# Two levels of 7-product multiplication for half of the gates in the last two groups, with the weight sums streamed from memory and the second sums of x made by GpSimd

## The chip, the core and the metric

The kernel runs on one core of a Trainium2 chip. A core has five engines that run side by side and wait for each other through semaphores: TensorE (PE in the profile, PEld for its weight loads), VectorE (DVE), ScalarE (ACT), GpSimd (POOL) and SyncE (SP, which here only issues transfers). The metric is the device time of one execution, in microseconds (us). Before the change the median of 3 executions was 768.82 us (767.99 to 770.23).

## The reference

```python
kv = einsum('bhsd,bhse->bhde', k, v)  # per batch and head: k^T v      (8 batches, 8 heads, 576 rows, 64 wide)
o  = q @ kv
x  = o / sqrt(mean(o*o) + 1e-6) * g  # then reshaped to 4608 rows x 512
a  = x @ w1                          # 512 -> 1024
b  = x @ w2                          # 512 -> 1024
h  = (a * b) @ w3                    # 1024 -> 1024
out = h @ w_out                      # 1024 -> 512
```

All values are float32. The two products `x @ w1` and `x @ w2` with the multiplication after them are called the gates here, and what follows them the projection; the kernel folds `w3 @ w_out` into one 1024 x 512 matrix at its start, so the projection is one product.

## The kernel before

**Groups.** The 4608 rows are worked on in nine groups of 512. Groups `T` = 0 to 7 hold 512 rows of batch `T`; group 8 holds the 64 rows left over of each batch. The order is 0, 1, ..., 6, 8, 7 (line 1100). For each group the gates are made in four blocks `p` = 0 to 3 (`gates`, line 742; each block is 128 features of the lower and 128 of the upper half, for w1 and w2), and then the projection (`project_twice`, line 859; group 0 uses `project`). Beside the gates of group `T` the attention of batch `T+1` is worked off in pieces (`steps`, called through `between`, line 1104), so the last two groups, 8 and 7, have no attention beside them.

**One level of 7 products.** A product of two matrices cut into 2 x 2 blocks can be made from 7 block products instead of 8, at the price of sums of blocks before and after. `winograd` (line 610) does so: the sums of weights s1 to s4 (`sums`), the sums of x t1 to t4 (`combine`) and the 7 products in the order (a11,b11), (s1,t1), (s2,t2), (s4,b22), (s3,t3), (a12,b21), (a22,t4). A block product of the gates is 4 matmuls of 128 x 128 weights by 256 rows (w1 and w2, two chunks of the contraction each), so a block `p` is 28 matmuls. The profile counts each float32 matmul as two instructions. `keep` (line 628) is ScalarE's copy of a product from PSUM to SBUF; `multiply` (line 747) adds two results on VectorE (line 756) and multiplies the two gates (line 757); the last result goes through a ScalarE copy and line 753. After each block, `sum_ab` (line 729) makes four sums of the finished gates, `ab`, for the projection (lines 670 and 671).

**Two levels in the projection.** `project_twice` cuts each of the 7 products again into 7: `sum_inner(n)` (line 844, lines 852 to 856) makes four sums of a left-hand block, `products(n)` (line 872) issues 7 x 2 matmuls of 128 x 128 by 128, and the results are kept (lines 905, 906), added (lines 933, 934, and 987) and finished on VectorE (`finish`, lines 915 to 918: one instruction of 128 elements a partition, three of 256). The second-level sums of the right-hand matrix were written to memory once by `prepare_b`, during group 1; `load_b` brings the 7 parts (896 KB each) of every group into three buffers in turn (`streams`), each as soon as the part three before it was used.

**Order.** TensorE, GpSimd and SyncE issue in the order of the program's text. VectorE does so from the last block of the gates to the end of the projection (`in_order`, line 1123); elsewhere the framework's scheduler orders VectorE and ScalarE. Each engine works strictly in its order, so an instruction that waits holds up all behind it. The chain that opens the projection is `following` (line 1114): after the result "c11" of block 3, VectorE makes the sums `sum_inner(0)`, which `products(0)` needs.

**Single buffers.** The tiles "p1", "p5", "u" (u2, u3 and u4 share it), "c" and "c21" of `late_pool` exist once each: a new `keep` into "u" waits until VectorE has read what is there. PSUM has five banks for "mm" and three for "at".

Of the kernel before, what the change touches and what calls it, by code (L numbers as in the profile page):

```python
# [2 lines left out]

# [8 lines left out]
FP32 = mybir.dt.float32  # L12
# [9 lines left out]
def kernel(  # L22
# [32 lines left out]
    nc = tc.nc  # L55
    PSUM = bass.MemoryType.PSUM
    P = 128

    B, H, S, D = q.shape
    DM = H * D  # L60
    DF = w1.shape[1]
    NP = H // 2
    KF = DF // P
    NH = KF // 2
    J = 4
    G = J * P
    N = G // 2
# [4 lines left out]
    const = ctx.enter_context(tc.tile_pool(name="const", bufs=1))  # L72
    inp = ctx.enter_context(tc.tile_pool(name="inp", bufs=2))
    work = ctx.enter_context(tc.tile_pool(name="work", bufs=2))
    ps_mm = ctx.enter_context(tc.tile_pool(name="ps_mm", bufs=5, space=PSUM))
    ps_at = ctx.enter_context(tc.tile_pool(name="ps_at", bufs=3, space=PSUM))
# [5 lines left out]
    def bank(pool, tag):  # L82
        return pool.tile([P, 512], FP32, name=tag, tag=tag)
# [31 lines left out]
    NF = KF // 2  # L115
# [141 lines left out]
    eps_col = const.tile([P, 1], FP32, name="eps_col")  # L257
    nc.vector.memset(eps_col, 1e-6)

    kv_sb = [const.tile([P, 2, NP, D], FP32, name=f"kv_sb{i}") for i in range(2)]  # L260
    g_col = const.tile([P, 1], FP32, name="g_col")


# [340 lines left out]
    late = {}  # L604
    tick = const.tile([P, 1], FP32, name="tick")

    def late_tile(name):
        return late_pool.tile([P, 7, P], FP32, name=name[0] if name[0] == "u" else name)
# [65 lines left out]
    def run(*step_lists):  # L674

        for steps in zip(*step_lists):
            for step in steps:
                step()
# [5 lines left out]
    PART = 7 * 2 * P  # L684
# [32 lines left out]
    def combine_x(T):  # L717
        xb[T] = {f"b{i + 1}{j + 1}": xT[T][:, i, j] for i in range(2) for j in range(2)}
        return combine(xb[T], parts(xc))
# [9 lines left out]
    def sum_ab(p):  # L729
        aa[p] = {f"a{i + 1}{j + 1}": ab[j][:, p, i, :] for i in range(2) for j in range(2)}  # L730
        return sums(aa[p], free["ab", p])
# [10 lines left out]
    def gates(T, p, between, ready=lambda name: None):  # L742
        def done(name, one, two):
            multiply(name, one, two)
            ready(name)

        def multiply(name, one, two):

            dst = ab[int(name[1]) - 1][:, p, int(name[2]) - 1, :]
            if two is None:  # L750
                c = late_pool.tile([P, N], FP32, name="c21")
                nc.scalar.copy(c, one[:, 0, :])
                nc.vector.tensor_mul(dst, c, one[:, 1, :])
                return
            c = late_pool.tile([P, 2, N], FP32, name="c")
            nc.vector.tensor_add(c, one, two)  # L756
            nc.vector.tensor_mul(dst, c[:, 0, :], c[:, 1, :])  # L757

        winograd(
            lambda name, w, c: wa[p][name][:, w, c, :],  # L760
            lambda name, c: xb[T][name][:, c, :],
            NP // 2, done, between,
        )


    def project(T, between):
        def done(name, one, two):
            half, j = int(name[1]) - 1, int(name[2]) - 1
            dst = o_sbs[half][:, :, j * N:(j + 1) * N]
            if two is None:  # L770
                nc.scalar.copy(dst, one)
            else:
                nc.vector.tensor_add(dst, one, two)
            if name in ("c11", "c21"):
                rows = out[T * S:T * S + G, :].rearrange("(p j) f -> p j f", j=J)
                nc.sync.dma_start(out=rows[:, 2 * half:2 * half + 2, :], in_=o_sbs[half])

        winograd(
            lambda name, m, p: aa[p][name][:, m * P:(m + 1) * P],
            lambda name, p: ob[p][name],  # L780
            NF, done, between,
        )
# [12 lines left out]
    def prepare_b():  # L795

        nc.sync.dma_start(
            out=w3o_l2[7, :, 0:1024].rearrange("p (f n) -> p f n", n=N), in_=b_blocks()[5]
        )
        for n, y in enumerate(b_blocks()):  # L800
            b11, b12, b21, b22 = (
                y[:, 2 * i:2 * i + 2, j * P:(j + 1) * P] for i in range(2) for j in range(2)
            )


            stage = w3o_sums[0].rearrange("p f n -> p (f n)") if n == 4 else (
                o_sbs[(n - n // 5) % 2].rearrange("p m n -> p (m n)")
            )
            stage = stage[:, 0:6 * P]
            t1, t2, t4 = (t.rearrange("p (c n) -> p c n", n=P) for t in (  # L810
                stage[:, i * 2 * P:(i + 1) * 2 * P] for i in range(3)
            ))
            nc.vector.tensor_sub(t1, b12, b11)
            nc.vector.tensor_sub(t2, b22, t1)
            nc.vector.tensor_sub(b12, b22, b12)
            nc.vector.tensor_sub(t4, b21, t2)
            nc.sync.dma_start(
                out=w3o_l2[n, :, 0:1024].rearrange("p (f n) -> p f n", n=N), in_=y
            )
            nc.sync.dma_start(out=w3o_l2[n, :, 1024:PART], in_=stage)  # L820
            yield
# [4 lines left out]
    def load_b():  # L826
        n = len(loaded_b)
        if n == ALL_B:
            return
        t = streams[n % len(streams)]  # L830

        part = {ALL_B - 2: 6, ALL_B - 1: 7}.get(n, n % 7)

        queue = nc.scalar if n % 7 in (3, 5) else nc.sync
        if n + 1 < ALL_B:
            queue.dma_start(out=t, in_=w3o_l2[part])
        else:
            t = t[:, 0:1024]
            queue.dma_start(out=t, in_=w3o_l2[part, :, 0:1024])
        loaded_b.append(t)  # L840
# [15 lines left out]
        nc.vector.tensor_sub(a21, a11, a21)  # L856
        inner[n] = [a11, a12, a22, s1, s2, s4, a21]

    def project_twice(T, last, ahead):
        def store(half):  # L860
            if T < B:
                rows = out[T * S:T * S + G, :].rearrange("(p j) f -> p j f", j=J)
# [118 lines left out]

            add(p5, r1)
        z = keep("u3", r1)
        load_b()
        if not last:
            sum_inner(6)
            nc.vector.tensor_add(p5, p5, z)
        finish(p5, 1, 1)
        products(6 if last else 5, r2)
        load_b()  # L990
        if last:
            add(z, r2)
            finish(z, 1, 0)
            last_block()
        else:
            add(p1, r2)
            finish(p1, 0, 0)
            products(6, r1)
            load_b()
            finish(keep("u4", r1), 1, 0)  # L1000

    done = {}
    dram = ctx.enter_context(tc.tile_pool(name="dram", bufs=1, space=bass.MemoryType.DRAM))
    w3o_l2 = dram.tile([8, P, PART], FP32, name="w3o_l2")


    ctx.enter_context(tc.manual_schedule(
# [93 lines left out]
    for n, T in enumerate(groups):  # L1101
        pieces = steps(T + 1) if n + 2 < NG else iter([])

        def between():
            next(pieces, lambda: None)()
            if T == 1:
                for _ in range(2):
                    if next(preparing, 0) == 0 and len(loaded_b) < 3:
                        load_b()

        for p in range(NF):
            if T and p + 1 == NF:
                sum_1, sum_2, sum_4, sum_3 = sum_ab(p)
                following = {
                    "c12": [], "c22": [sum_1],
                    "c11": [
                        lambda: sum_inner(0, lambda: all_of(f() for f in (sum_2, sum_3))),
                        lambda: sum_inner(1),
                    ],
                    "c21": [sum_4],  # L1120
                }

                in_order = tc.manual_schedule(engines={mybir.EngineType.DVE})
                in_order.__enter__()
                gates(T, p, between, lambda name: all_of(f() for f in following[name]))
                continue
            gates(T, p, between if T or p else lambda: None)
            if T == 0:
                if p + 1 < NF:
                    run(sum_w(p + 1))  # L1130
                for n in range(2):
                    if len(converted) < len(todo):
                        ahead = [copies["xT"] if p == 0 else copies["u3"][0], copies["u2"][p]][n]
                        with tc.issue_after(ahead.ins):
                            begin_next()
                        end_next()
                if p + 1 == NF:
                    allocate_projection()
                    run(*(f(i) for i in range(NF) for f in (sum_ab, combine_w3o)))
            else:  # L1140
                run(sum_ab(p))
        last = n + 1 == NG
        if T:
            project_twice(T, last, [] if last else combine_x(groups[n + 1]))
            in_order.__exit__(None, None, None)
            continue
        project(T, between)
        run(combine_x(1))
        preparing = prepare_b()
        third = late_pool.tile([P, 3, 2, P], FP32, name="inner_sums")  # L1150
        inner_sums.append([third[:, i] for i in range(3)])

# [29 lines left out]
```

## Time and profile before

| | |
|---|---|
| median of 3 executions | 768.82 us (767.99 to 770.23) |
| the profiled execution | 767.41 us |
| its span, first to last instruction | 765.4 us |
| TensorE busy | 758.5 us (99%), granted clock 0.999 |
| VectorE busy | 543.9 us (71%) |
| ScalarE busy | 253.3 us (33%) |
| GpSimd busy | 136.6 us (18%), none of it in the last two groups |
| gates of one block in the last two groups | 12.09 us |
| projection of one group (98 matmuls) | 21.89 us |

The page of a profile gives busy time by engine, the span in slices, the chain of work that ended last, and the costliest groups of instructions by source line. The timeline lists instructions in order of time: start, duration, engine, line, output and inputs, and in brackets the idle time of the engine before it with what ended it. A table of windows gives the busy time of each engine in stretches of the span. A matmul's shown duration is longer than the distance to the next one, since matmuls are pipelined; costs of TensorE are taken from the distance. On VectorE too the next instruction may start a little before the one ahead has ended, when it doesn't need its result.

### The profile page before, as it was taken

The page shows a single profiled execution, that of the slowest core. Times are in us where ns is not written, and L with a number is a line of the kernel's source. Part 1 is how long each engine was busy: PE and PEld are TensorE (multiplying, and loading weights), DVE is VectorE, ACT ScalarE, POOL GpSimd, SP SyncE. Part 2 cuts the span into 40 slices and gives each one's busy share as a digit, 9 for nine tenths or more (in the row PEclk, how much of TensorE's full clock was granted, in tenths as well). Part 3 has the DMA queues.
Part 4 walks back from the last instruction along what each step waited for, and adds up shares of the span by engine and source line. Part 5 has one row for each costly group of instructions (what it writes and reads, how often), then busy time and mean ns, then how long its engine had stood idle before and what let it go on. Part 6 is the DMA issues. An engine that isn't in the chain of part 4 may idle for free.

```text
span 765.4 us, 14413 instructions
## 1 busy us (share of the span) xinstructions
PE 758.5 (99%) x5775; PEld 660.1 (86%) x5775; DVE 543.9 (71%) x1083; ACT 253.3 (33%) x479; POOL 136.6 (18%) x132
## 2 busy tenths in 40 slices
PE   8999999999999999999999999999999999999998
PEld 6455788888899889988998899889988998898897
DVE  7978999548878578756775787667765864495467
ACT  6677763213222332223222321232133222222221
POOL 0000000222610351043113511331144000000000
PEclk9999999999999999999999999999999999999999
DMA  9996641339997844873487448844852470065015
GB/s 320 337 340 196 195 141 40 84 91 261 332 292 253 227 115 119 273 214 97 128 272 200 117 137 267 190 111 128 284 101 47 134 258 1 1 234 158 1 35 193
DMA packets 133159, 132.55 MB, mean 173 GB/s; under 512 B 76644, under 2 KB 121188, under 8 KB 133092
## 3 DMA queue, kind: packets, MB, share of 16 engines
q1 hardware_dynamic: 130640, 116.81, 52.5%
q10 hardware_dynamic: 2452, 14.81, 5.7%
q8 instruction: 46, 0.75, 0.4%
q14 instruction: 21, 0.17, 0.1%
HBM read 100.27 MB, written 16.38 MB: 152 GB/s over the span
## 4 chain that ended last, share of the span: by engine, by line
PE 97%; DMA 1%; ACT 0%; issue 0%; SPq 0%; DVE 0%; ACTq 0%
PE mm L617 60%; PE mm L894 23%; PE mm L596 7%; PE at L332 3%; PE at L415 2%; DMA raw<-in_moe_w_out_dram 1%; PE at L583 1%; PE at L351 1%; PE at L945 0%; DMA raw<-in_moe_w_dram 0%; PE at L449 0%; PE at L434 0%; ACT ab L157 0%; ACT chunks L158 0%; ACT kv_sb L343 0%; PE mm L434 0%
## 5 line engine op out<-in xcount | busy, mean ns | idle before, releaser
L617 PE MATMUL mm<-xT,w_sb 128*128 128x256 f32 x768 | 176.2, 379 | 0.0
L617 PEld LDWEIGHTS mm<-xT,w_sb 128*128 128x128 f32 x768 | 145.5, 190 | 20.0 <-issue 0.5
L617 PE MATMUL mm<-xc,ws 128*128 128x256 f32 x576 | 130.2, 379 | 0.0
L617 PEld LDWEIGHTS mm<-xc,ws 128*128 128x128 f32 x576 | 109.3, 190 | 15.0
L756 DVE TENSOR_TENSOR c<-mm,u 128x512 f32<-128x512 f32 x36 | 24.8, 689 | 103.3 <-PE mm L617 103.3
L630 ACT COPY u<-mm 128x512 f32<-128x512 f32 x74 | 43.4, 587 | 137.8 <-PE mm L617 129.2
L630 ACT COPY p<-mm 128x512 f32<-128x512 f32 x74 | 43.4, 586 | 88.0 <-PE mm L617 86.0
L617 PE MATMUL mm<-xc,w_sb 128*128 128x256 f32 x288 | 69.0, 382 | 0.0
L290 POOL COPY xT<-xn 128x1024 uint16<-128x1024 uint16 x26 | 31.7, 1249 | 173.0 <-DVE xn L393 173.0
L894 PE MATMUL mm<-w3o_sb,raw 128*128 128x128 f32 x500 | 62.4, 276 | 0.0
L596 PE MATMUL mm<-chunks,ab 128*128 128x512 f32 x128 | 60.3, 603 | 1.3 <-ACT ab L588 0.7
L757 DVE TENSOR_TENSOR ab<-c 128x256 f32<-128x256 f32 x108 | 59.1, 547 | 3.0
L617 PE MATMUL mm<-xT,ws 128*128 128x256 f32 x256 | 61.1, 381 | 0.0
L617 PEld LDWEIGHTS mm<-xc,w_sb 128*128 128x128 f32 x288 | 53.9, 190 | 7.7 <-ACT u L630 0.3
L894 PEld LDWEIGHTS mm<-w3o_sb,raw 128*128 128x128 f32 x500 | 59.0, 192 | 0.4 <-DVE raw L852 0.2
L617 PEld LDWEIGHTS mm<-xT,ws 128*128 128x128 f32 x256 | 48.0, 190 | 6.6
L384 DVE TENSOR_REDUCE inv<-sq 128x8 f32<-128x512 f32 (+1 forms) x40 | 23.4, 627 | 37.7 <-ACT sq L383 37.7
L756 DVE TENSOR_TENSOR c<-p,u 128x512 f32<-128x512 f32 x36 | 26.5, 736 | 27.5 <-ACT u L630 27.4
L894 PE MATMUL mm<-w3o_sb,ab 128*128 128x128 f32 x336 | 43.7, 275 | 0.0
L596 PEld LDWEIGHTS mm<-chunks,ab 128*128 128x128 f32 x128 | 21.8, 190 | 23.8 <-issue 15.8
L905 ACT COPY u<-mm 128x512 f32<-128x512 f32 x23 | 13.5, 587 | 85.7 <-DVE raw L918 63.2
L894 PEld LDWEIGHTS mm<-w3o_sb,ab 128*128 128x128 f32 x336 | 41.0, 192 | 0.3
(162 smaller groups left out, 1149.1 us busy)
## 6 DMA issues: line engine op xcount, KB each, us to landing
w3o_sb<-w3o_l SPq DMA_DIRECT2D x26, 896.0 KB, 4.9
raw<-in_moe_w_dram SPq DMA_DIRECT2D x31, 512.0 KB, 7.5
raw<-w3o_l SPq DMA_DIRECT2D x13, 896.0 KB, 5.2
w3o_sb<-w3o_l ACTq DMA_DIRECT2D x11, 896.0 KB, 4.6
k_sb<-in_k_dram SPq DMA_DIRECT2D x32, 256.0 KB, 4.0
v_sb<-in_v_dram SPq DMA_DIRECT2D x32, 256.0 KB, 4.6
q_sb<-in_q_dram SPq DMA_DIRECT2D x32, 256.0 KB, 4.4
out_dram<-raw SPq DMA_DIRECT2D x14, 512.0 KB, 3.5
```

The source lines that it names most:

```text
L290: nc.gpsimd.tensor_copy(to, src.rearrange("p a n w -> p w a n"))
L332: nc.tensor.matmul(kv_ps[e * D:(e + 1) * D, r - rs[0], :], lhsT=k_sb[:, e, cols] if j < J else kl[:, 2 * r + e, :], rhs=v_sb[:, e, cols] i ...
L351: nc.tensor.transpose(qt_ps[:, e, i, :], q_sb[:, e, i * P:(i + 1) * P], ident)
L384: nc.vector.tensor_reduce(out=inv[:, i], in_=sq.rearrange("p (h d) -> p h d", d=D), axis=AX.X, op=ALU.add)
L415: nc.tensor.matmul(o_ps[l][tokens, n * D:(n + 1) * D], lhsT=qT[r][rows, e, i, tokens], rhs=kv_b[rows, e, r, :], start=True, stop=True,)
L596: nc.tensor.matmul(sums_ps[half][m], lhsT=w3T[half, c][:, m, :], rhs=chunks[:, c, 1, :], start=(c == 0), stop=(c == KF - 1),)
L617: nc.tensor.matmul(ps[:, u, :], lhsT=lhsT(a_name, u, c), rhs=rhs(b_name, c),  start=(u == 0 and c == 0 and to is None), stop=(c == chunks ...
L630: copies.setdefault(name, []).append(nc.scalar.copy(t, ps))
L756: nc.vector.tensor_add(c, one, two)
L757: nc.vector.tensor_mul(dst, c[:, 0, :], c[:, 1, :])
L894: nc.tensor.matmul(to[:, i, :], lhsT=x[:, c, :], rhs=y[:, c, :], start=new and place // 4 not in seen, stop=(c == 1), skip_group_check=True,)
L905: nc.scalar.copy(t[:, 0:4], ps[0])
```

## The change

In the last two groups (`TWICE` = 8 and 7), blocks 0 and 1 of the gates are made together by two levels of 7 products. The contraction, the features and the rows are cut a second time: `gates_of_two` issues, for w1 and then w2, 7 outer times 7 inner products of one matmul each (128 x 128 by 128): 98 matmuls in place of 56. Its results are kept, added and finished as in the projection; for w2 a product with w1's result is added to each `finish`. The order of the blocks in these groups becomes 2, (0 and 1), 3; `sum_ab(0)` and `sum_ab(1)` come after the pair, ahead of block 3, and VectorE keeps the text's order from the pair on.

The second-level sums are made as follows. Those of the weights, 3 for each of 7 products, are made once by VectorE in `prepare_w`, called from `between` in blocks 0 and 1 of groups 3 and 4, and written to memory by 21 transfers of 128 KB; the fourth overwrites a weight block in group 6 (`replace_a21`). `load_w` brings them back in three parts of 896 KB, in place of the last three `load_b` of groups 6 and 8; those three `load_b` move into `gates_of_two`. The second sums of x, 28 subtractions of 128 x 128 for each group, are made by GpSimd (`sum_x`) during block 2 of the group, into tiles that attention used before. Two attention tiles become one (`kv_two`), which serves as another "u".

In the order that the built program has, the sums of `prepare_w` for products 0 and 1 (in group 3) and for 4 and 5 (in group 4; two times 3 instructions) stand on VectorE between the `finish` instructions of the projection before; those for products 2 and 6 stand before the two reductions of the attention's norm, and those for product 3 after the first addition of block 1. The subtractions of `replace_a21` stand around the four results of block 1 of group 6.

```diff
-    kv_sb = [const.tile([P, 2, NP, D], FP32, name=f"kv_sb{i}") for i in range(2)]
+    kv_two = const.tile([P, 2, 2, NP, D], FP32, name="kv_two")
+    kv_sb = [kv_two[:, i] for i in range(2)]
...
+    def w_blocks(name):
+        return [wa[m][name][:, :, c, :] for m in range(2) for c in range(2)]
+
+    def prepare_w():
+
+        for n, (name, _) in enumerate(PRODUCTS):
+            a11, a12, a21, a22 = w_blocks(name)
+            s1, s2, s4 = inner_sums[2 * (n % 2)]
+            nc.vector.tensor_add(s1, a21, a22)
+            nc.vector.tensor_sub(s2, s1, a11)
+            nc.vector.tensor_sub(s4, a12, s2)
+            for i, s in enumerate((s1, s2, s4)):
+                at = (3 * n + i) * 2 * P
+                nc.sync.dma_start(
+                    out=w_l2[:, at:at + 2 * P].rearrange("p (w m) -> p w m", w=2), in_=s
+                )
+            yield
+
+    def replace_a21():
+        for name, _ in PRODUCTS:
+            a11, _, a21, _ = w_blocks(name)
+            nc.vector.tensor_sub(a21, a11, a21)
+
+    loaded_w = []
+
+    def load_w():
+        n = len(loaded_w)
+        t = streams[(len(loaded_b) + n) % len(streams)]
+        nc.sync.dma_start(out=t, in_=w_l2[:, n * PART:(n + 1) * PART])
+        loaded_w.append(t)
...
+    def sum_x(T):
...
+        nc.gpsimd.tensor_copy(tick, late["p1"][:, 0, 0:1])
+        for t, (_, name) in zip(x_sums, PRODUCTS):
+            b11, b12, b21, b22 = (
+                xb[T][name][:, c, i * P:(i + 1) * P] for c in range(2) for i in range(2)
+            )
+            t1, t2, t3, t4 = t
+            nc.gpsimd.tensor_sub(t1, b12, b11)
+            nc.gpsimd.tensor_sub(t2, b22, t1)
+            nc.gpsimd.tensor_sub(t3, b22, b12)
+            nc.gpsimd.tensor_sub(t4, b21, t2)
...
+    def gates_of_two(T):
...
+            for place, x, y in (
+                (0, a11, b11), (3, a12, b21), (1, a22, t4), (2, s1, t1), (6, s2, t2), (5, s4, b22),
+                (4, s3, t3),
+            ):
+                nc.tensor.matmul(
+                    ps[place // 4][:, place % 4, :], lhsT=x, rhs=y,
+                    start=new and place // 4 not in seen, stop=True, skip_group_check=True,
+                )
+                seen.add(place // 4)
+            if w == 1 and n in (2, 4, 6):
+                load_b()
+            return ps
...
+        def finish(z, w, i, j):
...
+            dst = ab[i][:, 0:2, j, :].rearrange("p m (n t) -> p m n t", t=P)
+            to = dst
+            if w:
+                to = late_pool.tile([P, 2, N], FP32, name="c").rearrange("p m (n t) -> p m n t", t=P)
+            nc.vector.tensor_add(z[:, 6], z[:, 6], z[:, 0])
+            nc.vector.tensor_add(z[:, 4:6], z[:, 4:6], wide(6))
+            nc.vector.tensor_add(to[:, 1], z[:, 1:3], wide(4))
+            nc.vector.tensor_add(to[:, 0], z[:, 3:6:2], z[:, 0:3:2])
+            if w:
+                nc.vector.tensor_mul(dst, dst, to)
+
+        for w in range(2):
+            one = places["p1"] if w else late_tile("p1")
+            r1 = products(0, w, banks(ps_mm, "mm"), True)
+            p1 = keep(one, r1)
+            r2 = products(1, w, banks(ps_mm, "mm"), True)
+            p5 = keep(late_tile("p5"), r2)
+            products(2, w, r1, False)
+            z = keep(late_tile("u2"), r1)
+            products(3, w, r2, False)
+            add(z, r2)
+            finish(z, w, 0, 1)
+            products(4, w, r1, False)
+            u3 = keep(places["u"], r1)
+            nc.vector.tensor_add(p5, p5, u3)
+            finish(p5, w, 1, 1)
+            r3 = products(5, w, banks(ps_at, "at"), True)
+            add(p1, r3)
+            finish(p1, w, 0, 0)
+            products(6, w, r1, False)
+            finish(keep(late_tile("u4"), r1), w, 1, 0)
+        loaded_w.clear()
...
-        load_b()
+        load_after()
...
+            if T in (3, 4) and p < 2:
+                next(preparing_w, 0)
+            if T == B - 2 and p == 2 and not replaced:
+                replaced.append(True)
+                replace_a21()
+
+        if T in TWICE:
+            once = iter([T])
+            gates(T, 2, lambda: [sum_x(t) for t in islice(once, 1)])
+            run(sum_ab(2))
+            in_order = tc.manual_schedule(engines={mybir.EngineType.DVE})
+            in_order.__enter__()
+            gates_of_two(T)
+            run(sum_ab(0), sum_ab(1))
         for p in range(NF):
+            if T in TWICE and p + 1 < NF:
+                continue
...
-            project_twice(T, last, [] if last else combine_x(groups[n + 1]))
+            project_twice(
+                T, last, [] if last else combine_x(groups[n + 1]),
+                load_w if not last and groups[n + 1] in TWICE else load_b,
+            )
```

## The prediction

> **What bounds the kernel now.** I read the page's busy times and chain first, then a table of windows of group 7, then the timelines of TensorE and VectorE there.
>
> ```profile
> span 765.4 us, 14413 instructions
> PE 758.5 (99%) x5775; PEld 660.1 (86%) x5775; DVE 543.9 (71%) x1083; ACT 253.3 (33%) x479; POOL 136.6 (18%) x132
> PE 97%; DMA 1%; ACT 0%; issue 0%; SPq 0%; DVE 0%; ACTq 0%
> ```
>
> TensorE is the bound: the chain is 97% TensorE, so a saved matmul is saved time as long as nothing makes TensorE wait. Who would, shows in the windows (columns: stretch, then busy time of PE, PEld, DVE, ACT, POOL); first group 8's projection, then group 7's blocks 0 to 2:
>
> ```profile
> 669.52:691.41 21.89, 21.89 (x198) 21.88 (x196) 20.82 (x51) 5.12 (x10) 0.00 (x0) 1.00 0.70 235
> 691.41:703.50 12.09, 12.09 (x59) 10.64 (x57) 6.39 (x15) 2.83 (x5) 0.00 (x0) 1.00 0.65 196
> 703.50:715.60 12.10, 12.10 (x58) 10.65 (x57) 5.21 (x12) 2.72 (x5) 0.00 (x0) 1.00 0.00 0
> 715.60:727.70 12.10, 12.10 (x58) 10.65 (x57) 5.21 (x12) 2.72 (x5) 0.00 (x0) 1.00 0.01 1
> ```
>
> Two levels of 7 fill VectorE to 20.82 of 21.89 us; one level leaves it 7 us free in each block. The change turns two blocks of the second kind into a stretch of the first kind. The last view is the place where VectorE is nearly late already, the opening of group 7's projection:
>
> ```profile
> 738.66 0.68 DVE L756 TENSOR_TENSOR c<-mm,p 128x512 f32<-128x512 f32 x1
> 739.38 0.43 DVE L757 TENSOR_TENSOR ab<-c 128x256 f32<-128x256 f32 x1
> 739.84 0.42 DVE L852 TENSOR_TENSOR raw<-ab 128x256 f32<-128x256 f32 x1
> ...
> 741.77 0.41 DVE L856 TENSOR_TENSOR ab<-ab 128x256 f32<-128x256 f32 x1
> ...
> 739.76 1.50 PE L894 MATMUL mm<-w3o_sb,ab 128*128 128x128 f32 x12
> 741.10 1.50 PE L894 MATMUL mm<-w3o_sb,raw 128*128 128x128 f32 x12
> 742.44 0.61 PE L894 MATMUL mm<-w3o_sb,ab 128*128 128x128 f32 x4
> ```
>
> The last matmuls of `products(0)` start at 742.44 and read what line 856 ends at 742.18: 0.26 us of slack.
>
> **Part 1, TensorE: minus 4.58 us.** A block is 28 matmuls in 12.09 us (0.4318 each), a projection 98 in 21.89 (0.2233 each). Per group 56 of the first become 98 of the second: 24.17 to 21.89, minus 2.29, twice. All of it is on the path.
>
> [...]
>
> **Part 2, VectorE's backlog: plus 1.6 us a group.** Distances from group 8's and 7's timelines: a `finish` 1.46 us from its first start to the next instruction's (753.90 to 755.36), an addition of a PSUM pair 1.19 (752.71 to 753.90), an 896-element addition 1.12 (687.52 to 688.64), an independent 256-element sum 0.34. The new multiplication has 512 elements: 0.60 (676.56 to 677.17), plus 0.12 since line 918's successor now waits for its result. For w1 VectorE has two pairs, one 896 addition and four finishes: 2.38 + 1.12 + 5.84 = 9.34 us. For w2 four multiplications of 0.72 more: 12.22. The eight sums of `sum_ab(0)` and `(1)`: 2.7.
>
> Times from the start of the pair: an inner product set is 7 x 0.2233 = 1.563 us. w1's work can start at 5.85 (the first bank of its fourth set, plus 0.27, VectorE's lag behind TensorE in the rows) and ends at 15.2; w2's starts at 10.94 + 5.85 = 16.8 and, with the sums, ends at 31.7. TensorE left the pair at 21.9. In block 3 the first addition (line 756) could start at 21.89 + 4 x 1.727 + 0.27 = 29.06, so it is 2.6 us late. Who waits: ScalarE's `keep("u3")`, since "u" exists once. Addition until 32.4, copy 0.59 until 33.05, then TensorE's set (a22,t4), due at 32.25: a stall of about 0.9. VectorE goes on: u3's addition, multiplication, sum, "c11", its multiplication (2.72 from 737.12 to 739.84 in the rows) and 2.35 from line 852's start to line 856's end: 33.07 + 2.72 + 2.35 = 38.14. The last pair of `products(0)` is due at 33.97 + 0.9 + 2.68 = 37.55: another 0.7. Together 1.6 a group, 3.2 in all. After that VectorE is as far behind TensorE as now, and the rest of the projection has over 1 us of slack. Bounds: each distance could be off by 2% of the 21 us that the chain runs, and a stalled TensorE may take some tenths to restart: 1.2 to 2.2 a group.
>
> **Part 3, GpSimd's sums: nothing taken.** 28 subtractions of 128x128 with two inputs; no such row exists. From below: the one-input 128x128 instruction of the identity, 0.295 us; from above: twice that, 0.59, for two inputs read in turn. I take 0.42, nearer the lower end, since GpSimd's rows of 512 and 1024 elements (0.67 and 1.2) put 0.13 on every instruction whatever its size. They start after the `tick`, 2.7 us into block 2 (keep of p1 ends 2.5 in, 693.93; tick 0.19), and last 11.8. They also take turns with VectorE:
>
> ```profile
> 585.69 0.86 DVE L756 TENSOR_TENSOR c<-p,u 128x512 f32<-128x512 f32 x1
> 586.58 1.14 DVE L757 TENSOR_TENSOR ab<-c 128x256 f32<-128x256 f32 x1
> 585.95 1.50 POOL L292 COPY qT_left<-xn_left 128x1024 uint16<-128x1024 uint16 x1
> ```
>
> Line 757 takes 0.42 with GpSimd idle and 1.14 beside it; additions that read PSUM are not touched (0.69 at 583.97). About eight such VectorE instructions of block 2 cost GpSimd 3.4 us, so the last sums stand at 17.9; they are needed at 12.09 + 6 x 1.563 + 0.45 = 21.9. Covered by 4 us. At 0.59 they end at 22.6, and past 18 us VectorE's finishes of w1 interleave: up to 4 us of stall a group. VectorE's side of it, up to 2.5 us late at "c11" of block 2, frees a PSUM bank that TensorE wants 2.5 us into the pair: covered, barely (0 to 0.5 a group).
>
> [...]
>
> **Part 4, groups 3 and 4: plus 0.6 us.** Six of the weight sums stand between finishes of the projection before. In the gaps of dependent instructions they delay the end of p1's finish by 1.3 us, not 2.0 (six slots of 0.34, less what the gaps gave). It ended at 320.78, so 322.1; ScalarE's keep of p1 then runs 322.2 to 322.8, and TensorE wants that bank at 319.29 + 3.45 = 322.74: 0.1 a group. The three sums ahead of the norm's reductions meet GpSimd's copies (331.91 and 407.35, 2.2 us): each may wait 0.7 to 0.8, so the reductions come 2 to 2.6 us late, ScalarE's square root behind them too, and behind that stands keep of p1 of block 1. In group 3 it still ends in time (337.15 against 337.44); in group 4 it misses 412.88 by 0.4. Sum 0.6; bounds 0 and 3 (these sums also overwrite buffers that transfers of 128 KB, 3.2 us to landing in the rows, must have left). SyncE's 21 transfers wait for the sums; queued behind are loads of k, v and q that land a block ahead of use: nothing.
>
> **Part 5, the rest: nothing.** `replace_a21`'s first four subtractions stand before block 1's first addition in group 6 (568.32); u3's copy waits for TensorE until 569.97, so 0.9 us is free, against 0.34 and one turn with GpSimd: 0 to 0.5. `load_w` and the moved `load_b` land in about 5 us (rows: 4.5 to 5.2), with at least 10 between freed buffer and use.
>
> **Sum.** -4.58 + 3.2 + 0.6 = -0.8 us. The profiled execution took 767.41 (span 765.4 and 2 around it), 1.4 below the median. So about 766.6 there, and 768.0 as a median. Bounds together: -4.58 + 2.4 = -2.2, and -4.58 + 4.4 + 3 + 1.5 = +4.3.
>
> **Rivals.**
> - *The backlog costs nothing:* the full 4.58, 764.2 us. It needs VectorE's chain 2.6 us shorter; all its distances are measured in the same shapes. Or, in part, a shorter one.
> - *GpSimd is too slow (the one on the other side):* place, the sets of w1, whose t-sums aren't there. It decides from about 0.55 us a subtraction, with price up to 4 a group: +6 to +8, about 774. For it: no row has the price; against it: one-input rows are 0.2 to 0.3.
> - *The sums in groups 3 and 4 hold VectorE up* in front of the norm, by GpSimd's turns and by transfers that have not left the buffers: 2 to 2.5 a group, so 772. For it: VectorE's strict order; against: about 2 us of slack behind it on ScalarE.
> - *The pair runs slower than the projection's pace:* against it, the same shapes at 0.2233 in the projections of groups 6 and 8.
>
> **Chances.** Forecast 0.58, almost all of it within 0.3% (2.3 us, about what a measurement of this kernel tells from no change); backlog free 0.12; GpSimd 0.14; groups 3 and 4 0.12; pace 0.04. So faster 0.13, same 0.59, slower 0.28. The range leaves out the full gain and the dearest half of the GpSimd case: 765.6 to 773.5; the forecast's own is 766.6 to 771.
>
> **What the profile will show.** Right: 98 matmuls of a pair at 0.223; idle TensorE of 0.5 to 1 us before (a22,t4) of block 3 and within `products(0)`, in both groups, VectorE busy without a gap from 17 us into the pair; GpSimd done about 6 us into it. Wrong: TensorE waiting for GpSimd in the pair, a GpSimd subtraction above 0.55, no stall in block 3, or stalls over 1 us in groups 3 and 4.

## The result and the profile after

Six executions of the changed kernel gave 768.07 us in the median (767.57 to 769.74), six of the kernel before 768.61 us (766.88 to 770.23); the ratio is 0.9995, with a 95% interval of 0.9978 to 1.0012. The two can't be told apart. The profiled execution of the changed kernel took 769.74 us, 1.7 above its median. First the page of the changed kernel (span, busy time by engine, the chain that ended last):

```profile
span 767.9 us, 15002 instructions
...
PE 757.6 (99%) x5943; PEld 660.6 (86%) x5943; DVE 586.2 (76%) x1175; ACT 262.9 (34%) x499; POOL 164.6 (21%) x190
...
PE 81%; issue 6%; DVE 6%; DMA 4%; POOL 2%; ACT 0%; SPq 0%; POOLq 0%; ACTq 0%; DVEq 0%
```

VectorE is busy for 42 us more (543.9 before), and the chain, 97% TensorE before, now passes through VectorE and other engines too. Its shares are not what their work costs, since TensorE is still busy for 99% of the span. Where TensorE loses time, the table of windows shows: group 8's projection, then group 7's block 2, the pair, and block 3 (columns as before: length, then busy time of PE, PEld, DVE, ACT, POOL); the last line is group 7's block 3 in the kernel before.

```profile
671.83:694.39 22.56, 22.41 (x197) 22.03 (x196) 21.42 (x51) 5.11 (x10) 0.00 (x0) 1.00 0.68 228
694.39:706.48 12.09, 12.09 (x58) 10.65 (x57) 6.79 (x15) 2.82 (x5) 9.12 (x20) 1.00 0.65 197
706.48:728.36 21.88, 21.88 (x197) 21.88 (x196) 16.63 (x37) 10.32 (x20) 4.67 (x10) 1.00 0.23 77
728.36:741.51 13.15, 12.63 (x58) 10.48 (x57) 12.49 (x30) 2.94 (x6) 0.00 (x0) 1.00 0.25 84
...
727.70:739.76 12.06, 12.06 (x58) 10.61 (x56) 5.17 (x12) 2.72 (x5) 0.00 (x0) 1.00 0.00 1
```

The pair takes 21.88 us instead of 24.17. Block 3 takes 13.15 instead of 12.09, with VectorE busy for 12.49 of it (5.17 before), and the projection 22.56 instead of 21.88. All stretches that differ, each from its first matmul to the first of the next stretch:

| stretch, us | before | after | difference |
|---|---|---|---|
| blocks of group 3 | 53.56 | 53.69 | +0.13 |
| blocks of group 4 | 54.38 | 55.60 | +1.22 |
| group 8: blocks 0 and 1 | 24.17 | 21.88 | -2.29 |
| group 8: block 3 | 12.09 | 13.14 | +1.05 |
| group 8: projection | 21.88 | 22.56 | +0.68 |
| group 7: blocks 0 and 1 | 24.17 | 21.88 | -2.29 |
| group 7: block 3 | 12.09 | 13.15 | +1.06 |
| group 7: projection and last block | 22.38 | 23.06 | +0.68 |
| sum | | | +0.24 |

Two more stretches differ in these two profiles, but move about in all 14 profiles of this study, though the work there is nearly the same: the one up to the first product with `kv` (57.99 before, 59.40 after; 57.66 to 59.40 over all) and the projection of group 1 (22.49 and 23.28; 22.28 to 23.79, mostly waits for a part of w3o). Loads of w3o also hold up another projection now and then, by 0.4 to 1.2 us. So times vary by some 2 us where the stretches above repeat within 0.05, and the experiments are read by these stretches first.

Where the time goes in block 3 and in the first product set of group 7's projection, in the timeline:

```profile
735.06 0.58 ACT L632 COPY u<-mm 128x512 f32<-128x512 f32 x1 [2.41 <-DVE c L883]
...
735.70 3.72 PE L619 MATMUL mm<-xT,w_sb 128*128 128x256 f32 x16 [0.26 <-ACT u L632]
...
738.27 0.68 DVE L758 TENSOR_TENSOR c<-mm,u 128x512 f32<-128x512 f32 x1
...
739.04 0.58 ACT L632 COPY u<-mm 128x512 f32<-128x512 f32 x1 [3.40 <-DVE c L758]
...
739.68 1.99 PE L619 MATMUL mm<-xc,w_sb 128*128 128x256 f32 x8 [0.27 <-ACT u L632]
...
744.30 0.42 DVE L999 TENSOR_TENSOR ab<-ab 128x256 f32<-128x256 f32 x1
...
744.77 0.71 PE L1037 MATMUL mm<-w3o_sb,ab 128*128 128x128 f32 x4
```

Block 3's first addition (line 758) starts at 738.27, 31.79 us after the pair's first matmul; 31.7 was forecast. TensorE waits twice in block 3: for the copy of u2, which waited for the pair's last `finish` (line 883) to be done with the one "u" tile, and for the copy of u3, which waited for line 758. Each shows 0.26 to 0.27 us of idle time and lengthens the block by about 0.53. From the pair's last `finish` to line 758 VectorE is busy without a gap.

### The profile page after: what moved, and what is told of

Its sections match the earlier page's. It is cut to its first block, busy times and chain, and to the rows that moved or that the text cites. A ratio compares the mean times of both kernels' runs of the same rounds, so it can differ in the third digit from the quotient of the medians.

```text
span 767.9 us, 15002 instructions
## 1 busy us (share of the span) xinstructions
PE 757.6 (99%) x5943; PEld 660.6 (86%) x5943; DVE 586.2 (76%) x1175; ACT 262.9 (34%) x499; POOL 164.6 (21%) x190
## 3 DMA queue, kind: packets, MB, share of 16 engines
HBM read 105.78 MB, written 19.14 MB: 163 GB/s over the span
## 4 chain that ended last, share of the span: by engine, by line
PE 81%; issue 6%; DVE 6%; DMA 4%; POOL 2%; ACT 0%; SPq 0%; POOLq 0%; ACTq 0%; DVEq 0%
PE mm L619 44%; PE mm L1037 18%; PE mm L598 8%; PE mm L850 4%; PE at L334 2%; PE at L417 2%; DMA w3o_sb<-w3o_l 1%; PE at L585 1%; DMA w_l<-raw 1%; DMA q_sb<-qT 1%; DMA xn<-xT 1%; DMA raw<-in_moe_w_out_dram 1%; DVE ab L885 1%; POOL xT L306 1%; POOL qT L306 1%
## 5 line engine op out<-in xcount | busy, mean ns | idle before, releaser
L619 PE MATMUL mm<-xT,w_sb 128*128 128x256 f32 x720 | 165.3, 379 | 0.3 <-ACT u L632 0.3
L619 PEld LDWEIGHTS mm<-xT,w_sb 128*128 128x128 f32 x720 | 136.2, 190 | 19.3 <-ACT u L632 0.7
L619 PE MATMUL mm<-xc,ws 128*128 128x256 f32 x512 | 116.2, 380 | 0.8 <-ACT p L632 0.8
L619 PEld LDWEIGHTS mm<-xc,ws 128*128 128x128 f32 x512 | 97.0, 190 | 14.9 <-ACT p L632 1.8
L632 ACT COPY u<-mm 128x512 f32<-128x512 f32 x66 | 38.6, 586 | 126.2 <-PE mm L619 106.0
L292 POOL COPY xT<-xn 128x1024 uint16<-128x1024 uint16 x26 | 31.2, 1227 | 179.2 <-DVE xn L395 179.2
L632 ACT COPY p<-mm 128x512 f32<-128x512 f32 x66 | 38.5, 584 | 74.0 <-PE mm L619 68.3
L619 PE MATMUL mm<-xc,w_sb 128*128 128x256 f32 x256 | 61.6, 383 | 0.5 <-ACT u L632 0.5
L759 DVE TENSOR_TENSOR ab<-c 128x256 f32<-128x256 f32 x96 | 53.3, 555 | 2.5
L619 PEld LDWEIGHTS mm<-xc,w_sb 128*128 128x128 f32 x256 | 47.7, 190 | 8.1 <-ACT u L632 1.6
L1048 ACT COPY u<-mm 128x512 f32<-128x512 f32 x23 | 13.5, 586 | 86.7 <-DVE raw L1061 50.5
L306 POOL COPY xT<-xn 128x1024 uint16<-128x1024 uint16 x26 | 30.9, 1218 | 52.0 <-DMA xn<-xT 52.0
```

The source lines that it names most:

```text
L292: nc.gpsimd.tensor_copy(to, src.rearrange("p a n w -> p w a n"))
L306: nc.gpsimd.tensor_copy(words(dst), src)
L619: nc.tensor.matmul(ps[:, u, :], lhsT=lhsT(a_name, u, c), rhs=rhs(b_name, c),  start=(u == 0 and c == 0 and to is None), stop=(c == chunks ...
L632: copies.setdefault(name, []).append(nc.scalar.copy(t, ps))
```

## The experiments

The theory: VectorE has more to do from the pair's w2 to the projection than TensorE's time there, and this debt eats 1.74 of the 2.29 us a group; besides, the weight sums cost 1.35 us in groups 3 and 4. Rivals: the single "u" tile, ScalarE's copies or GpSimd's sums cause the waits in block 3, or the stalls in groups 3 and 4 come and go by chance.

### VectorE's debt: 2.7 us taken out

```diff
-            run(sum_ab(0), sum_ab(1))
+            sum_ab(0), sum_ab(1)
```

> Left out: in the last two groups the eight sums of 256 elements over the gates of feature blocks 0 and 1 (two times sum_ab), so the output of these groups is not the reference's. It takes 2.7 us out of VectorE's chain between the pair and block 3 and changes nothing else. Theory (VectorE's backlog): the first addition of block 3 starts 2.7 us earlier, on time; the waits of TensorE in block 3 and in the first product set of the projection, 1.74 us a group, go; time 3.5 us less, 764.6. Rival (the waits come from ScalarE's copies or from GpSimd, not from the length of VectorE's chain): they stay, 768.1.

Measured: 766.97 us against 768.83, ratio 0.9975 (0.9962 to 0.9988). Block 3 12.62 us in both groups, the projection back to 21.88. So 1.20 us a group went, not 1.74: the projection's wait and that for u3 are VectorE's debt, but 0.53 in block 3 stayed. It is the wait for u2's copy (0.27 us of idle time in each group, as before); it hangs on the pair's last `finish`, which comes before these sums in VectorE's order, and I had not forecast it.

### The tiles: u3, then u2, in a tile of its own

```diff
-            t = late_tile(name)[:, 0:4, :].rearrange("p (u a) n -> p u (a n)", u=2)
+            t = own_u3[0] if name == "u3" and own_u3 else late_tile(name)
+            t = t[:, 0:4, :].rearrange("p (u a) n -> p u (a n)", u=2)
```

(`own_u3` holds `places["u"]` during block 3 of the last two groups; the second kernel does the same for "u2".)

> In block 3 of the last two groups u3 is kept in a tile of its own, so its copy need not wait for VectorE's addition that still reads u2. Theory (VectorE's backlog is the cost, the shared tile only the first place where it shows): the two waits of 0.25 us in block 3 go, VectorE gets through its chain only about 0.3 us earlier, and the waits within the first product set of the projection grow from 1.2 to about 1.45 us a group; in all 0.3 a group, so 767.5. Rival (the shared tile is the cost): 0.52 a group go and the waits in the projection stay as they are, 767.0 or below; if the whole wait hung on the tile, 3.5 us go, 764.6.

> In block 3 of the last two groups u2 (not u3) gets a tile of its own, which neither the last finish of the pair nor the addition of c12 reads. Theory (VectorE's chain is what is late, the tile only shows it): block 3 takes 12.09 us instead of 13.14, so both its waits go, but VectorE's chain ends only 0.25 to 0.3 us earlier and the first product set of the projection waits 1.35 to 1.5 us instead of 0.68; in all 0.3 us a group, 767.5. Rival (the tile is the cost): 1.05 a group, 766.0. Rival (the addition of c12 frees a bank that TensorE wants in block 3): block 3 stays above 12.5.

Own u3: block 3 12.62 us (0.52 less), projection 22.96 (0.40 more); that is 0.12 in all in group 8 (0.15 in group 7), 768.94 us against 768.83, ratio 0.9995 (0.9978 to 1.0011). The waits of TensorE in the last two groups of this kernel (idle time in total, times, longest):

```profile
PE mm L1040 <- DVE ab L762: 0.9, 2, 0.4
...
PE mm L621 <- ACT u L635: 0.5, 2, 0.3
```

One wait for u is left in each group, and the projection now waits up to 0.4 us for VectorE's multiplication of c11 (line 762, formerly 759). Own u2: block 3 is 12.09 again, both waits gone; the projection takes 23.47, 0.91 more than in the changed kernel; 0.14 a group, 767.71 us against 767.97, ratio 0.9992 (0.9978 to 1.0006). The rival falls: with VectorE this late, a tile only decides where TensorE pays. The theory's 0.3 a group was too much, since VectorE gained even less by not waiting for u3. (The 1.2 us that the first text gives for the projection's waits as they were is 0.68 by the table above.)

### The weight sums in another place

```diff
-            if T in (3, 4) and p < 2:
+            if T in (2, 3, 4, 5) and p == 1:
                 next(preparing_w, 0)
```

> The seven steps of weight sums (three VectorE sums and three transfers each) move from blocks 0 and 1 of groups 3 and 4 to block 1 of groups 2 to 5, behind the norm instead of between the projection's finishes and in front of the norm's reductions. Theory (the sums hold the norm up): in the changed kernel TensorE lost 0.12 us in group 3 and 1.22 us in block 1 of group 4; both go, the first copy of p in block 1 of group 4 starts again about 0.2 us after its matmul, and the time falls by about 1.3 us, to some 766.8. The waits of the last two groups stay at 1.74 us each. Rival (these waits come and go from run to run, whatever the place of the sums): the wait of 0.8 us for p in group 4 stays, time as in the changed kernel, 768.1.

Measured: 768.21 us against 768.83, ratio 0.9991 (0.9980 to 1.0003). Group 4 fell from 55.60 to 54.53, but group 3 stayed at 53.69 and group 2 rose from 54.38 to 55.17. The timeline at group 2's start shows why:

```profile
245.84 0.42 DVE L778 TENSOR_TENSOR raw<-w_sb,raw 128x256 f32<-128x256 f32 x1
246.18 0.42 DVE L1060 TENSOR_TENSOR raw<-p 128x256 f32<-128x256 f32 x1
246.52 0.42 DVE L1061 TENSOR_TENSOR raw<-p 128x256 f32<-128x256 f32 x1
...
247.03 1.07 ACT L632 COPY p<-mm 128x512 f32<-128x512 f32 x2 [2.82 <-DVE raw L1061]
...
247.67 0.48 PE L619 MATMUL mm<-xc,ws 128*128 128x256 f32 x1 [0.52 <-ACT p L632]
```

Written in block 1, the sums (lines 776 to 778) were drawn forward by the scheduler into the gaps of p1's `finish` (lines 1058 to 1061) of the projection before: they wait for nothing. The copy of p1 then waits for line 1061. The edit didn't do what it says, so the next holds the sums back in issue order.

```diff
-            if T in (3, 4) and p < 2:
-                next(preparing_w, 0)
+            turns[T, p] = turns.get((T, p), 0) + 1
+            if T in (2, 3, 4, 5) and p == 1 and turns[T, p] == 2:
+                with tc.issue_after(copies["c"][-2].ins):
+                    next(preparing_w, 0)
+                    next(preparing_w, 0)
```

(`copies["c"]` collects the additions of `multiply`; the last but one is c22's.)

> The weight sums are held back in issue order: two steps (six VectorE sums, six transfers) in block 1 of each of groups 2 to 5, queued behind that block's c22 addition, so that the scheduler can't draw them forward into the projection's finishes or in front of the norm. Theory (they cost because VectorE reaches p1's finish, or the norm's reductions, later): all stretches of blocks in groups 2 to 6 take as long as in the kernel before; the 0.13 of group 3 and the 1.22 of group 4 go, and nothing like the 0.79 us of the previous run's group 2 comes; 1.35 us less than in the changed kernel, 766.7. Rival (transfers of the sums or the extra VectorE work cost wherever they stand): stalls of 0.1 to 1 us in blocks 1 or 2 of groups 2 to 5, 767.5 to 768.

Measured: 767.12 us against 767.97, ratio 0.9989 (0.9979 to 1.0000). All stretches of groups 2 to 6 as in the kernel before to 0.01 us, 1.35 less than in the changed kernel, with the same sums and transfers. It is their place in VectorE's order that costs.

### How far GpSimd is from mattering

```diff
+            for _ in range(2):
+                nc.gpsimd.tensor_sub(t1, b12, b11)
...
```

> GpSimd makes each of its 28 subtractions twice, same operands and results. Theory (GpSimd has about 5 us of slack: it ended 4.8 us into the pair, and the last sums are wanted 9.8 us into it): 28 more at 0.45 us are 12.6 us, the last sums come 17 us into the pair unless VectorE delays them further, TensorE waits 6 to 7 us a group in the product sets of w1, time up by 12 to 14 us, to 781. Rival (the sums are wanted later, or GpSimd's second subtraction overlaps): 0 to 3 us a group, below 775. Rival (the turns with VectorE's finishes stretch both engines): over 9 us a group, above 786.

Measured: 788.71 us against 768.83, ratio 1.0256 (1.0226 to 1.0286). The pair took 31.31 us in group 8 and 32.57 in group 7, 9.4 and 10.7 more. The rival of the turns was right, in time (over 786) and in mechanism: the last sums came 19.1 and 19.2 us into the pair, not 17, since subtractions beside VectorE's finishes took up to 0.68 us in the mean of four, in place of 0.45. The first matmul that reads the last product's sums (tile qT) shows it, first in the changed kernel's group 8, then in this kernel's groups 8 and 7:

```profile
646.62 0.39 PE L850 MATMUL mm<-qT,w_sb 128*128 128x128 f32 x2
...
654.01 0.49 PE L851 MATMUL mm<-qT,w_sb 128*128 128x128 f32 x2 [0.49 <-POOL qT L822]
...
733.28 0.79 PE L851 MATMUL mm<-qT,w_sb 128*128 128x128 f32 x2 [0.49 <-POOL qT L822]
```

It starts 9.82 us after the pair's first matmul in the changed kernel, here 19.14 and 19.29: 9.3 and 9.5 us of the loss are GpSimd's lateness. TensorE's idle time for GpSimd adds up to only 6.6 and 6.2 us, mostly because TensorE also ran at half its clock for a while, in windows of group 8's and group 7's pair (the column before the DMA share is the granted clock):

```profile
634.86:646.92 12.06, 8.57 (x73) 8.18 (x72) 5.90 (x12) 4.18 (x9) 11.59 (x25) 1.00 0.00 0
646.92:653.75 6.83, 4.00 (x18) 3.41 (x16) 5.14 (x9) 0.47 (x1) 6.59 (x14) 0.50 0.00 0
...
725.43:735.67 10.24, 7.54 (x34) 6.95 (x34) 6.15 (x11) 1.57 (x3) 7.56 (x15) 0.50 0.00 1
735.67:746.56 10.89, 10.89 (x99) 10.89 (x99) 6.36 (x14) 5.22 (x10) 0.00 (x0) 1.00 0.47 154
```

In group 8 the half clock ended at 653.75, before the last sums were there, so it filled time in which TensorE would have waited for them anyway. In group 7 it lasted 2.4 us beyond their arrival, which accounts for the other 1.2 us.

### The debt moved, or given to GpSimd

All mended in order: the weight sums behind c22, u2's tile, and the gate sums moved behind the first inner sums.

```diff
-            run(sum_ab(0), sum_ab(1))
+            two = [sum_ab(0), sum_ab(1)]
...
+                    one, second, fourth, third_sum = zip(*two, sum_ab(p))
+                    following = {
+                        "c12": [], "c22": [sum_1],
+                        "c11": [
+                            lambda: sum_inner(0, to=inner_a21[0]), *one[:2],
+                            lambda: sum_inner(1, lambda: all_of(f() for f in second)),
+                        ],
+                        "c21": [],
+                    }
+                    left = {2: fourth, 4: third_sum}
```

(`left[2]` runs within `sum_inner(2)`, `left[4]` ahead of `sum_inner(4)`; `inner_a21` is a tile of `sum_x` that is free then.)

> Three edits together: the weight sums behind block 1's c22 addition as above, a tile of its own for u2, and the twelve sums over the gates (blocks 0, 1 and 3) of the last two groups moved from between pair and block 3 into the projection, behind its first inner sums, each ahead of its first reader. Theory (the matmul saving of 2.29 us a group is real and only covered by VectorE's backlog): pair 21.89, block 3 12.09, projection 21.89 to 22.2 in both groups; the last two groups lose 4.1 to 4.58 us against the kernel before, groups 2 to 6 nothing; time 764.3, from 764.0 to 765.0. Rival (VectorE's total work in these two groups is the bound, so the backlog only moves on): new waits of 1 to 2 us a group later in the projection or in block 2 of the next group, 766 to 767.5.

Measured: 767.61 us against 767.97, ratio 0.9990 (0.9980 to 0.9999). Groups 2 to 6 as before the change and block 3 at 12.09, but group 8's projection 23.79, group 7's block 2 12.32, its projection 23.46, and 1.1 us more between the last matmul and the end. The rival was right (767.61 is just above its 766 to 767.5). The timeline near the end:

```profile
752.95 0.68 DVE L1081 TENSOR_TENSOR u<-mm,u 128x512 f32<-128x512 f32 x1
...
753.69 1.60 PE L1042 MATMUL mm<-w3o_sb,ab 128*128 128x128 f32 x12 [0.82 <-DVE u L1081]
...
760.54 0.42 DVE L1066 TENSOR_TENSOR raw<-u 128x256 f32<-128x256 f32 x1
760.88 0.74 DVE L1098 TENSOR_TENSOR raw<-raw,at 128x256 f32<-128x256 f32 x2
```

The debt comes out late in the projection, and the kernel now ends on VectorE's work. So the sums go to GpSimd, idle there:

```diff
-            run(sum_ab(0), sum_ab(1))
+            run(sum_ab(0, nc.gpsimd), sum_ab(1, nc.gpsimd))
```

> The eight sums of 256 elements over the gates of feature blocks 0 and 1 in the last two groups are made by GpSimd, which is idle there, instead of VectorE; nothing else changes. Leaving them out gave 1.20 us a group. Estimate of one on GpSimd: 0.77 us (0.13 fixed, 0.32 for 128 elements in the rows), 6.2 us in all, beside VectorE's work in block 3. Theory (the two engines take turns at instructions that touch only SBUF): about nine such VectorE instructions in block 3 lose 0.2 to 0.4 us each, so most of the 2.7 us that VectorE saves goes back; block 3 stays between 12.6 and 13.2, the projection between 22.2 and 22.8; 0 to 0.6 us a group, 767.0 to 768.1. Rival (the engines run beside each other): block 3 12.62, projection 21.88 as when the sums were left out, 2.4 us in all, 765.7.

Measured: 769.10 us against 768.87, ratio 1.0003 (0.9993 to 1.0013). Block 3 13.85 us, worse than forecast, projection 22.11, better; 0.26 lost in group 8, 0.22 in group 7. In group 8:

```profile
661.88 0.94 DVE L881 TENSOR_TENSOR u<-u 128x256 f32<-128x256 f32 x1
662.85 0.83 DVE L882 TENSOR_TENSOR c<-u 128x256 f32<-128x256 f32 x1
...
664.13 0.59 ACT L632 COPY u<-mm 128x512 f32<-128x512 f32 x1 [3.64 <-DVE c L883]
...
664.76 3.72 PE L619 MATMUL mm<-x_left,w_sb 128*128 128x256 f32 x16 [1.49 <-ACT u L632]
```

Beside GpSimd's sums (1.41 us for two in a row, at times 1.59 or 1.60) VectorE's additions of 256 elements took 0.83 and 0.94 us, 0.42 without. Each lost 0.41 to 0.52 us, less than one GpSimd sum takes. Then the combinations:

> Two edits together: the weight sums behind block 1's c22 addition, and a tile of its own for u2 in block 3 of the last two groups. Theory (the two gains are independent): groups 2 to 6 as in the kernel before, the last two groups 139.6 us against 141.0; 1.4 us less than the kernel before and 1.6 less than the changed kernel, ratio 0.998, 766.4. Rival (VectorE's lateness moves into the following group or the end, as when the gate sums were moved): no gain beyond the 1.1 us that holding the sums back gives, 766.9.

The two mends together (diffs above): 767.17 us against 768.87, ratio 0.9976 (0.9967 to 0.9986). Groups 2 to 6 378.15 us as in the kernel before, the last two groups 139.59 against 140.96: 1.4 less than before, 1.6 less than the changed kernel, as expected.

> The two mends (weight sums behind c22, a tile of its own for u2) and, with them, the eight gate sums of blocks 0 and 1 on GpSimd. Alone the move to GpSimd lost 0.26 us a group, since its turns held up the last finish of the pair, which u2's copy waited for; with its own tile u2 does not wait for that. Theory (the turns cost VectorE about half of the 2.7 us, the rest is gained): block 3 12.09, projection of group 8 22.6 to 22.9 instead of 23.49, so 0.6 to 0.9 us a group; 138.1 us for the last two groups, time about 1.4 us below the two mends alone, 2.8 below the kernel before. Rival (the turns eat all of it): projection 23.3 or more, no gain over the two mends.

766.76 us against 768.45, ratio 0.9978 (0.9969 to 0.9988); group 8's projection 23.58, the last two groups 139.79. My theory fell: of VectorE's 2.7 us the turns with GpSimd left nothing.

> As the last, and block 3's own sums s2, s3 and s4 move from in front of the projection's first inner sums to just ahead of their readers (the first inner sums write their last block elsewhere). VectorE's total work is that of the last kernel. Theory (the debt of VectorE at the start of the projection is now about 0.9 us, and the projection has about that much slack further on): projection 21.9 to 22.3, last two groups 136.7 to 137.3, time 3.7 us below the kernel before, ratio 0.995. Rival (VectorE's total is the bound, as when all gate sums were moved): the waits come again later in the projection or as a longer tail at the end, 138 us or more with the tail.

Here block 3's own sums move behind the first inner sums too, in the manner of the diff with `left`:

```diff
+                            lambda: sum_inner(0, to=inner_a21[0]), lambda: sum_inner(1, sum_2),
...
+                    left = {2: [sum_4], 4: [sum_3]}
```

766.45 us against 768.45, ratio 0.9973 (0.9962 to 0.9983); the last two groups 139.11, and 0.24 more in the tail. Again far from the 137 hoped for, and the rival's 138 or more is met: TensorE waits 1.1 us at the start of each projection, for c11's multiplication, which GpSimd's turns in block 3 made late.

### The whole saving, with the debt gone

The two mends, and the eight sums left out:

> The two mends (weight sums behind c22, a tile of its own for u2) and the eight gate sums of blocks 0 and 1 of the last two groups left out, so that the output of these groups is not the reference's: 2.7 us less work for VectorE in each group, on no other engine. Theory (the saving on TensorE is whole, and it is VectorE's 2.7 us that eat what is left of it): block 3 12.09, projection 21.88 to 22.1, last two groups 136.4 to 136.8 us against 141.0 before, 4.2 to 4.6 us less than the kernel before, 763.8 to 764.3. Rival (some other wait, of a bank or a load, holds block 3 or the projection once VectorE is early): 137.4, as when the sums alone were left out, or more; 765 or more.

Measured: 763.73 us against 768.44, ratio 0.9932 (0.9911 to 0.9954); the last two groups 136.38 us, 4.58 less than before. Group 8's pair, block 3 and projection:

```profile
633.62:655.51 21.89, 21.89 (x198) 21.89 (x197) 16.66 (x37) 10.32 (x20) 4.70 (x10) 1.00 0.23 78
655.51:667.60 12.09, 12.09 (x59) 10.64 (x58) 10.61 (x23) 2.93 (x6) 0.00 (x0) 1.00 0.26 90
667.60:689.48 21.88, 21.88 (x197) 21.88 (x196) 20.75 (x50) 5.12 (x10) 0.00 (x0) 1.00 0.71 237
```

TensorE is busy without a gap in all three. The saving is whole once VectorE has 2.7 us less to do and u2 has its own tile: the theory of the debt stands. The tile has a share of its own, though. With the eight sums alone left out the last two groups took 137.45 us, so without the debt it is worth 0.53 a group, beside the debt only 0.14.

## Why the prediction was right, point by point

- *Part 1, -4.58.* Exact: 98 matmuls in 21.88 us in both pairs, 0.2233 each, and 4.58 in the last experiment.
- *Part 2, +1.6 a group.* Measured 1.74 (1.05 and 0.68). VectorE's chain was right to 0.1 us: line 758 at 31.79 after 31.7, the end of line 999 (line 856 before) at 38.24 after 38.14, and 0.68 in `products(0)` after 0.7. The stall in block 3 is nearly right too (1.05 after 0.9), but not where it falls: the set (a22,t4) started 33.20 us after the pair's first matmul, where a copy that ends at 33.05 was forecast, and the delay came as two waits of 0.53, u3's and before it u2's. The step "who waits: ScalarE's `keep("u3")`, since "u" exists once" overlooked that u4 of the pair is a "u" as well, so that block 3's u2 waits for the pair's last `finish`. By these rows the wait adds next to nothing beside the debt, since VectorE reaches line 758 no later for it and u3's copy hangs on that line; without the debt it stays (0.53 when the eight sums were left out). The 0.7 in `products(0)` also splits: 0.31 fell already on c11's multiplication (line 759), which the forecast doesn't name, and 0.37 on line 999.
- *Part 3, nothing.* Right. A subtraction took 0.45 to 0.46 us alone (0.42 assumed) and up to 0.91 beside VectorE, past the 0.55 that was to be a sign of being wrong. Alone, the next started after 0.41 or, where it needs the result, 0.53. The last ended 16.95 us into group 8's block 2 (17.9 forecast), and no matmul of the pair waited:

```profile
627.67 0.45 POOL L818 TENSOR_TENSOR k_sb<-x_left 128x128 f32<-128x128 f32 x1
628.20 0.46 POOL L819 TENSOR_TENSOR k_sb<-x_left,k_sb 128x128 f32<-128x128 f32 x1
628.61 0.45 POOL L820 TENSOR_TENSOR k_sb<-x_left 128x128 f32<-128x128 f32 x1
...
641.20 0.46 POOL L821 TENSOR_TENSOR qT<-xc,qT 128x128 f32<-128x128 f32 x1
```

- *Part 4, +0.6.* Mis-sized: 1.35. The "0.1 a group" at p1's copy is right (0.13 and 0.1); the "0.4 in group 4" is about 1.1. The timeline of the changed kernel in group 4:

```profile
410.40 0.71 DVE L776 TENSOR_TENSOR raw<-w_sb 128x256 f32<-128x256 f32 x1 [1.09 <-DMA w_l<-raw]
411.04 1.25 DVE L673 TENSOR_TENSOR raw<-raw,ab 128x256 f32<-128x256 f32 x1
412.21 1.25 DVE L673 TENSOR_TENSOR ab<-ab 128x256 f32<-128x256 f32 x1
...
414.17 1.27 DVE L386 TENSOR_REDUCE inv<-sq 128x8 f32<-128x512 f32 x2
...
415.69 1.05 ACT L632 COPY p<-mm 128x512 f32<-128x512 f32 x2
...
416.31 1.99 PE L619 MATMUL mm<-xc,ws 128*128 128x256 f32 x8 [0.83 <-ACT p L632]
```

  A sum waited 1.09 us for a transfer to leave its buffer. I had named that wait and priced it only as a bound. And it pushed two sums of the gates (line 673; 0.42 each at 406.89 and 407.24 before) behind the start of GpSimd's copies, where they took 1.25. The reductions came 3.5 us later in their group, not 2 to 2.6.
- *Part 5, nothing.* Right: block stretches of groups 5 and 6 unchanged; after group 1 no wait of TensorE for a load shows in the changed kernel.
- *Sum.* -0.8 forecast; +0.24 in the stretches, -0.5 between medians. The stretches are 1.0 worse than forecast, 0.75 of it from Part 4. That the forecast median of 768.0 lies within 0.1 of the measured 768.07 is luck, with times that vary by some 2 us. Of the rivals, GpSimd's slowness was off by more than I said: it decides above 0.55 us a subtraction by the text, but 0.46 left about 5 us, 0.18 for each of 28, so nearer 0.63 by this profile (an estimate from 16.95 against 21.9).

## What to carry to other kernels

A saving on the engine that bounds the kernel is worth what the next engine leaves of it: sum that engine's work from the place where it stops having gaps to the next place where it has some, and expect the excess as waits. Here moving the work within that stretch, or giving a buffer of its own to whoever waits, mostly moved the waits. Less work took away all but 0.53 us a group of them, and with less work the tile took away that too. Work that waits for nothing goes where the scheduler puts it, not where the text has it, so pin it behind an instruction. The two mends (the sums pinned, u2's tile) give 0.9976 of the kernel before, with the same arithmetic.

## What the hardware showed that I had not expected

TensorE's granted clock fell to 0.50 for 6.83 and 10.24 us in the kernel with twice the subtractions, each time after waits of 1.4 and 2.1 us with 1.8 us of matmuls between them: 1.4 us after the second wait in group 8, 0.8 in group 7. Through both waits it was still at 1.00. The two spells are two and three times as long as one of 3.41 us near the start of the changed kernel (at 11.66). The waits of 0.26 and 0.27 us in the changed kernel's block 3 left the clock at 1.00. What makes it fall, these runs don't show. Two GpSimd sums of 128 x 256 in a row took 1.41 us, about 0.7 each, where VectorE takes 0.42 for one. What VectorE saved by handing over eight of them came back as its lost time (139.79 us against 139.59 for the last two groups), so idle GpSimd is no spare VectorE here.
